# Loading the first layer's weights in two column parts in a deep cross network kernel

## Chip, cores, metric

One core of a Trainium2 chip. The metric is the device time of one execution in microseconds, median over runs. The profile's span is about 1.8 us shorter than that time. Changes of less than 2% (9.5 us here) count as "same"; this study is about fractions of a microsecond at the very start, so single executions are looked at closely.

## The reference

```python
B, Din, L = 16384, 416, 6             # x0: [B, Din], ws: [L, Din, Din], bs: [L, Din], all bfloat16
x = x0
for l in range(L):
    proj = x @ ws[l] + bs[l]
    x = x0 * proj + x
```

## The kernel before

The batch is cut into 8 groups of 2048 rows, a group into 4 chunks of 512. Features lie on partitions: 416 = 3 x 128 + 32, so a layer's output has three full tiles (0, 1, 2) and a tail of 32. TensorE is kept busy by a hand-made order of (group, layer) jobs. A helper, `add(engine, fn, reads, writes, lane)`, derives the semaphore waits from named tokens; a DMA has its own lane and semaphore.

Only the start matters here. SyncE issues every load of it, in this order:

```python
def load_wm(l, eng):                       # 384 rows x 832 B = 312 KB, one DMA
    add(eng, lambda h: h.dma_start(wm[l][:, :, :], ws[l, 0:NT * P, :].rearrange("(t p) f -> p t f", p=P)),
        writes=[("wm", l)], lane=f"wm{l}", batch=0)
...
load_nat(0, 0, 2)                          # rows of chunk 0, first half (208 KB)
load_nat(0, 2, KK)                         # second half
load_wm(0, "sp")
for j in range(1, NJ):                     # rows of chunks 1, 2, 3, in halves
    load_nat(j, 0, 2)
    load_nat(j, 2, KK)
load_w3(0, "sp")                           # the last 32 weight rows, four copies
load_group(1)                              # DMA transposes of the next group
```

The first job, group 0 in layer 0, turns its rows on TensorE, because a DMA transpose would come too late (the first one of this trace, for group 1, is issued at 7.25 us and lands at 12.67):

```python
keep_busy(25, 7)                           # filler matmuls
transposed_chunk(0)                        # 12 transposes, then copies PSUM -> SBUF by VectorE and ScalarE
... biases; keep_busy(5, 3)
full(g, l, 0, ba, True, True, chunks=[0])  # tile 0, chunk 0: first main matmuls, need the weights
full(g, l, 1, bb, True, True, chunks=[0])  # tile 1, chunk 0
transposed_chunk(1)
transposed_chunk(2)
full(g, l, 0, ba, True, True, chunks=[1])
full(g, l, 1, bb, True, True, chunks=[1])
transposed_chunk(3)
transposed_tails(7)
full(g, l, 0, ba, True, True, chunks=[2, 3])
rows32(g, l, 0, ba, False)                 # small rows of tile 0
...                                        # tile 1; then tile 2 for all chunks, tails, second job
```

Of the kernel before, what the change touches and what calls it, by code (L numbers as in the profile page):

```python
# [3 lines left out]
P = 128  # L4
# [17 lines left out]
class Program:  # L22
# [12 lines left out]
    def add(self, eng, fn, reads=(), writes=(), lane=None, batch=None, hold=False, release=False):  # L35
        op = Op(eng, fn, lane, batch)
        deps = {}
        if eng == "pool":
            writes = list(writes) + ["pool"]
        for t in reads:  # L40
            w = self.writer.get(t)
            if w is not None:
                deps[id(w)] = (w, True)
        for t in writes:
            w = self.writer.get(t)
            if w is not None:
                deps[id(w)] = (w, True)
            for r in self.readers.get(t, ()):
                if id(r) not in deps:
                    deps[id(r)] = (r, False)  # L50
        for d, raw in deps.values():
            if d.lane is None and d.eng == eng and lane is None and (eng == "pe" or not raw):
                continue
            op.deps.append(d)
        for t in reads:
            self.readers.setdefault(t, []).append(op)
        for t in writes:
            self.writer[t] = op
            self.readers[t] = []
        if eng == "dve":  # L60
            if hold:
                self.flush()
                self.held = op
            else:
                self.queue[eng].append(op)
                if release:
                    self.flush()
        else:
            self.queue[eng].append(op)
        if lane is not None:  # L70
            batches = self.lanes.setdefault(lane, [])
            if not batches or batches[-1][0] != batch:
                batches.append((batch, []))
            batches[-1][1].append(op)
        return op
# [123 lines left out]
def bass_standalone__cross_network_dcn__recsys_kernel(  # L199
# [6 lines left out]
    B, D = x0.shape  # L206
    L = ws.shape[0]
    NT = 3
# [24 lines left out]
    wm = [nc.alloc_sbuf_tensor(f"wm_{l}", [P, NT, D], BF16) for l in range(L)]  # L233
# [17 lines left out]
    add = pr.add  # L251
# [4 lines left out]
    def x0_tok(s, t, j):  # L256
        return ("x0", s, t, j)
# [7 lines left out]
    def slot(g):  # L265
        return g % NX0

    def bank(b, p0=0, p1=P, n=CH):
        return psum[p0:p1, b * CH:b * CH + n]
# [3 lines left out]
    def take(n):  # L273
        got = [(ring[0] + i) % 8 for i in range(n)]
        ring[0] = (ring[0] + n) % 8
        return got


    def load_wm(l, eng):
        add(eng, lambda h: h.dma_start(wm[l][:, :, :], ws[l, 0:NT * P, :].rearrange("(t p) f -> p t f", p=P)),  # L280
            writes=[("wm", l)], lane=f"wm{l}", batch=0)

    def load_w3(l, eng):
        for j in range(NJ):
            add(eng, lambda h, j=j: h.dma_start(w3[l][j * T32:(j + 1) * T32, :], ws[l, NT * P:D, :]),
                writes=[("w3", l, j)], lane=f"w3{l}", batch=0)

    def load_group(g):
        s = slot(g)
        rows = slice(g * GC, (g + 1) * GC)  # L290
        def turn(t):
            add("sp", lambda h: h.dma_start_transpose(
                x0s[s][:, t * GC:(t + 1) * GC], x0[rows, t * P:(t + 1) * P]),
                writes=[x0_tok(s, t, j) for j in range(NJ)], lane=f"x0_{s}_{t}", batch=g)

        turn(0)
        add("sp", lambda h: h.dma_start_transpose(Tb, x0[rows, D - P:D]),
            writes=[("ost", t, j) for t in range(NT + 1) for j in range(NJ)], lane="Tb", batch=g)
        turn(1)
        turn(2)  # L300
        if g > 1:
            for j in range(NJ):
                q = slice(j * T32, (j + 1) * T32)
                add("sp", lambda h, q=q, j=j: h.dma_start(
                    x0s[s][q, XW:XW + CH], Tb[P - T32:P, j * CH:(j + 1) * CH]),
                    reads=[("ost", 0, 0)], writes=[("x03q", s, j)], lane=f"x03_{s}", batch=g)
            rotate_x03(g)

    def rotate_x03(g):
        s = slot(g)  # L310
        if turn_of(g, 1):
            rotate(x0s[s][:, XW:XW + CH], x0s[s][:, XW + CH:XW + 2 * CH], turn_of(g, 1),
                   x03_toks(s), ("x03r", s), f"x03r_{s}", g)
# [9 lines left out]
    def quad(g, l, j):  # L323
        q = (j + turn_of(g, l)) % NJ
        return q, slice(q * T32, (q + 1) * T32)
# [14 lines left out]
    def x_src(g, l):  # L340

        if l == 0:
            s = slot(g)
            return lambda t, a, b: x0s[s][:, t * GC + a * CH:t * GC + b * CH], lambda t, j: x0_tok(s, t, j)
        s = xset[(g, l)]
        return lambda t, a, b: xs[s][:, t * GC + a * CH:t * GC + b * CH], lambda t, j: ("x", s, t, j)

    def x3_src(g, l):
        if l == 0:
            s = slot(g)  # L350
            return x0s[s][:, XW:XW + CH], x03_toks(s)
        s = xtail[(g, l)]
        return x3s[s][:, :], [("x3", s)]

    def done_with(g, l):
        users[(g, l)] = users.get((g, l), 0) + 1
        if users[(g, l)] < 2:
            return
        if l > 0:
            free_x.append(xset[(g, l)])  # L360
            free_3.append(xtail[(g, l)])
        prefill(g, l + 1)
        if l == L - 1:
            output(g)
            if g == 3:
                load_last()
            if 4 < g + NX0 <= LAST:
                load_group(g + NX0)
# [90 lines left out]
    def full(g, l, i, banks, first, chunk_major, after_chunk=None, chunks=range(NJ), ts_=range(NT)):  # L459
        src, stok = x_src(g, l)  # L460
        ecols = slice(i * P, (i + 1) * P)
        seq = [(t, j) for j in chunks for t in ts_] if chunk_major else \
              [(t, j) for t in ts_ for j in chunks]
        for t, j in seq:
            n = 1
            if (g, l) in HALVES and halves[0] and t != (0 if first else NT - 1):
                halves[0] -= 1
                n = 2
            w = CH // n
            for k in range(n):  # L470
                add("pe", lambda h, t=t, j=j, k=k, w=w: h.matmul(  # L471
                    bank(banks[j])[:, k * w:(k + 1) * w], wm[l][:, t, ecols], src(t, j, j + 1)[:, k * w:(k + 1) * w],
                    start=(first and t == 0), stop=(not first and t == NT - 1)),
                    reads=[stok(t, j), ("wm", l)], writes=[("ps", banks[j])])
            if after_chunk and t == NT - 1:
                after_chunk(j)

# [20 lines left out]
    def tails(batch):  # L498
        bs_ = take(len(batch))
        for (g, l), b in zip(batch, bs_):  # L500
            s3, tok3 = x3_src(g, l)
            for j in range(NJ):
                (ri, qi), (ro, qo) = quad(g, l, j), quad(g, l + 1, j)
                add("pe", lambda h, l=l, b=b, s3=s3, ri=ri, qi=qi, ro=ro, qo=qo: h.matmul(  # L504
                    psum[qo, b * CH:(b + 1) * CH], w3[l][qi, NT * P:D], s3[qi, :],
                    start=True, stop=False, tile_position=(ri * T32, ro * T32)),
                    reads=tok3 + [("w3", l, ri)], writes=[("ps", b)])
        for (g, l), b in zip(batch, bs_):
            src, stok = x_src(g, l)
            for t in range(NT):  # L510
                for j in range(NJ):
                    ro, qo = quad(g, l + 1, j)
                    add("pe", lambda h, t=t, j=j, src=src, l=l, b=b, ro=ro, qo=qo: h.matmul(  # L513
                        psum[qo, b * CH:(b + 1) * CH], wm[l][:, t, NT * P:D], src(t, j, j + 1),
                        start=False, stop=(t == NT - 1), tile_position=(0, ro * T32)),
                        reads=[stok(t, j), ("wm", l)], writes=[("ps", b)])
            evacuate_tail(g, l, b)
        pr.flush()
        for g, l in batch:
            done_with(g, l)  # L520
# [15 lines left out]
    def load_nat(j, k0, k1):  # L536
# [6 lines left out]
        reads=["warm"], writes=["warm"])  # L543
    load_nat(0, 0, 2)
    load_nat(0, 2, KK)
    load_wm(0, "sp")
    for j in range(1, NJ):
        load_nat(j, 0, 2)
        load_nat(j, 2, KK)
    load_w3(0, "sp")  # L550
    load_group(1)

    def second_tails():
# [106 lines left out]
    def job_banks():  # L660
        return take(NJ)
# [159 lines left out]
    for n, it in enumerate(items):  # L821
# [11 lines left out]
        if mode[n] in ("FR", "F1"):  # L833
            banks = job_banks()
# [3 lines left out]
        else:  # L838
            banks = job_banks()
# [13 lines left out]
    g, l = LAST, L - 1  # L853
    src, stok = x_src(g, l)
# [161 lines left out]
```

## Time and profile before

| | before |
|---|---|
| time, median of 3 runs | 475.73 us (475.69 to 475.93) |
| span of the profile | 473.9 us |
| TensorE busy | 467.7 us (99%) |
| TensorE waiting for the first weights | 1.02 us |
| first weights issued, landed | 1.65, 6.08 us |
| first main matmul | 6.21 us |

TensorE is the bound. What can be won by removing a wait is the idle time of TensorE, 6.2 us in all, and the wait for the first weights is the largest item of it inside the stream. The profile lines that show this stand in the prediction.

### The profile page before, as it was taken

Reading aid. Unit: us, or ns where it says so; the run is one execution under the profiler, and the core shown is the slowest. Engines: PE = TensorE matmul, PEld = TensorE weight load, DVE = VectorE, ACT = ScalarE, POOL = GpSimd, SP = SyncE. Lnnn points to the kernel's source line nnn. Section 1 sums busy time; section 2 is a strip of 40 time slices with the busy share of each in tenths; the row PEclk is TensorE's granted clock in tenths of the full one; section 3 lists DMA queues with packets and bytes.
Section 4 is the critical chain, followed back from the end, with each engine's and each line's share of the span. In section 5 each row is a group of like instructions: output and inputs, shape, how many; then the busy total and the mean of one; then the engine's idle time right before and its main releaser. Section 6 shows DMA issues by size and latency. Waiting matters only on the chain.

```text
span 473.9 us, 8467 instructions
## 1 busy us (share of the span) xinstructions
PE 467.7 (99%) x3408; PEld 199.5 (42%) x3408; DVE 404.5 (85%) x700; ACT 340.9 (72%) x371; POOL 6.0 (1%) x15
## 2 busy tenths in 40 slices
PE   8999999999999999999999999999999999999996
PEld 4344445654444444444444444444444444444442
DVE  2888888888888888898888869888888888888897
ACT  4677777777777777777777777777777777777775
POOL 1000000000000000000000000000000000001000
PEclk9999999999999999999999999999999999999999
DMA  8995910740102388369319930880001039026999
GB/s 227 183 183 136 212 46 1 134 90 1 35 0 46 72 233 142 76 151 228 89 25 190 228 92 19 201 247 1 1 10 27 0 61 237 26 46 102 226 173 290
DMA packets 138651, 53.18 MB, mean 112 GB/s; under 512 B 112362, under 2 KB 138100, under 8 KB 138612
## 3 DMA queue, kind: packets, MB, share of 16 engines
q1 hardware_dynamic: 138456, 52.54, 49.8%
q8 instruction: 26, 0.43, 0.4%
q14 instruction: 13, 0.11, 0.1%
q10 hardware_dynamic: 156, 0.11, 0.1%
HBM read 5.97 MB, written 13.63 MB: 41 GB/s over the span
## 4 chain that ended last, share of the span: by engine, by line
PE 94%; DMA 2%; DVE 2%; ACT 1%; SPq 0%; issue 0%; DVEq 0%
PE ps L471 78%; PE ps L492 7%; PE ps L513 7%; PE ps L486 1%; DMA wm<-in_ws_dram 1%; DVE x L931 1%; DVE x L925 1%; DMA x<-x 1%; ACT tw L398 1%; PE ps L504 1%; DMA ot<-x 1%; PE ps L591 0%; DVE tw L407 0%; SPq L537 0%; ACT ost L709 0%
## 5 line engine op out<-in xcount | busy, mean ns | idle before, releaser
L398 ACT ACTIVATE tw<-ps,bias 128x1024 bf16<-128x1024 f32 (+1 forms) x295 | 299.5, 1070 | 119.8 <-PE ps L492 80.1
L471 PE MATMUL ps<-x,wm 128*128 128x512 bf16 (+1 forms) x1755 | 379.6, 372 | 1.0 <-DMA wm<-in_ws_dram 1.0
L471 PEld LDWEIGHTS ps<-x,wm 128*128 128x128 bf16 x1755 | 165.1, 98 | 209.7 <-issue 28.2
L407 DVE TENSOR_TENSOR tw<-tw,x 128x1024 bf16<-128x1024 bf16 (+1 forms) x285 | 192.6, 683 | 52.5 <-ACT tw L398 52.0
L412 DVE TENSOR_TENSOR x<-tw,x 128x1024 bf16<-128x1024 bf16 (+1 forms) x285 | 182.4, 680 | 0.0
L492 PE MATMUL ps<-x,w 32*128 32x512 bf16 x512 | 39.2, 379 | 0.0
L513 PE MATMUL ps<-x,wm 128*32 128x512 bf16 x564 | 33.0, 380 | 0.0
L438 ACT ACTIVATE ts<-ps,bias 128x512 bf16<-128x512 f32 x47 | 28.7, 700 | 0.0
L442 DVE TENSOR_TENSOR x<-ts,x 128x512 bf16<-128x512 bf16 x47 | 18.6, 417 | 3.2 <-DMA x<-x 3.1
L513 PEld LDWEIGHTS ps<-x,wm 128*32 128x32 bf16 x564 | 13.8, 96 | 17.5 <-issue 5.2
L492 PEld LDWEIGHTS ps<-x,w 32*128 32x128 bf16 x512 | 7.8, 92 | 26.9 <-issue 26.4
L440 DVE TENSOR_TENSOR ts<-ts,x 128x512 bf16<-128x512 bf16 x47 | 18.5, 417 | 0.0
L711 POOL COPY ost<-ot 128x512 bf16<-128x512 bf16 x6 | 4.6, 766 | 422.9 <-DMA ot<-x 422.9
L867 PE MATMUL ps<-wm,x 128*128 128x416 bf16 x48 | 9.7, 340 | 0.0
L601 DVE COPY x<-ps 128x512 bf16<-128x512 bf16 x5 | 2.0, 422 | 8.6 <-PE ps L591 8.5
L919 ACT ACTIVATE x<-ps 128x416 bf16<-128x416 f32 x16 | 7.7, 517 | 2.1 <-PE ps L867 2.0
L603 ACT ACTIVATE x<-ps 128x512 bf16<-128x512 bf16 x7 | 3.8, 595 | 5.3 <-PE ps L591 5.3
L867 PEld LDWEIGHTS ps<-wm,x 128*128 128x128 bf16 x48 | 4.2, 98 | 4.4 <-issue 1.0
L504 PE MATMUL ps<-x,w 32*32 32x512 bf16 x188 | 5.9, 374 | 0.0
L486 PE MATMUL ps<-x,w 32*32 32x512 bf16 x208 | 5.7, 385 | 0.0
L931 DVE TENSOR_TENSOR x<-x,x 128x832 bf16<-128x832 bf16 (+1 forms) x9 | 4.7, 540 | 0.2
L925 DVE TENSOR_TENSOR x<-x,x 128x832 bf16<-128x832 bf16 (+1 forms) x10 | 4.8, 498 | 0.0
(40 smaller groups left out, 32.3 us busy)
## 6 DMA issues: line engine op xcount, KB each, us to landing
out_dram<-ost SPq DMA_DIRECT2D x6, 1664.0 KB, 7.0
x<-x SPq DMA_DIRECT2D x24, 96.0 KB, 2.1
wm<-in_ws_dram SPq DMA_DIRECT2D x6, 312.0 KB, 3.3
x<-in_x_dram SPq DMA_DIRECT2D x8, 208.0 KB, 4.2
x<-in_x_dram SPq DMA_DIRECT2D x4, 416.0 KB, 8.3
out_dram<-ost SPq DMA_DIRECT2D x2, 832.0 KB, 5.4
x<-x SPq DMA_DIRECT2D x22, 64.0 KB, 2.0
out_dram<-x SPq DMA_DIRECT2D x3, 416.0 KB, 4.3
```

The costliest lines, as they stand in the source:

```text
L398: add("act", lambda h, a=a, w=w, b0=b0: h.activation(tw[r][:, a * CH:(a + w) * CH], psum[:, b0 * CH:(b0 + w) * CH], ACT_F.Identity, bias=b ...
L407: add("dve", lambda h, a=a, e=e: h.tensor_tensor(tw[r][:, a * CH:e * CH], tw[r][:, a * CH:e * CH], x0s[s0][:, i * GC + a * CH:i * GC + e * ...
L412: add("dve", lambda h, a=a, e=e: h.tensor_tensor(xs[so][:, i * GC + a * CH:i * GC + e * CH], tw[r][:, a * CH:e * CH], src(i, a, e), ALU.ad ...
L438: add("act", lambda h: h.activation(ts[r][:, :], bank(b), ACT_F.Identity, bias=bias[:, 3, l:l + 1], scale=1.0), reads=[("ps", b), "bias"], ...
L440: add("dve", lambda h: h.tensor_tensor(ts[r][:, :], ts[r][:, :], x03, ALU.mult), reads=[("ts", r)] + tok0, writes=[("ts", r)], release=True)
L442: add("dve", lambda h: h.tensor_tensor(x3s[so][:, :], ts[r][:, :], res, ALU.add), reads=[("ts", r)] + rtok, writes=[("x3", so), ("x3", so, ...
L471: add("pe", lambda h, t=t, j=j, k=k, w=w: h.matmul(bank(banks[j])[:, k * w:(k + 1) * w], wm[l][:, t, ecols], src(t, j, j + 1)[:, k * w:(k ...
L486: add("pe", lambda h, q=q, j=j, r=r, c=c, o=o: h.matmul(psum[o, banks[j] * CH:(banks[j] + 1) * CH], w3[l][q, i * P + c * T32:i * P + (c + ...
L492: add("pe", lambda h, q=q, j=j, r=r: h.matmul(bank(banks[j]), w3[l][q, ecols], src[q, :], start=first and not inner, stop=not first and no ...
L504: add("pe", lambda h, l=l, b=b, s3=s3, ri=ri, qi=qi, ro=ro, qo=qo: h.matmul(psum[qo, b * CH:(b + 1) * CH], w3[l][qi, NT * P:D], s3[qi, :], ...
L513: add("pe", lambda h, t=t, j=j, src=src, l=l, b=b, ro=ro, qo=qo: h.matmul(psum[qo, b * CH:(b + 1) * CH], wm[l][:, t, NT * P:D], src(t, j, ...
L867: add("pe", lambda h, t=t: h.matmul(bank(b, n=D), xcol(t, j, kk), wm[l][:, t, :], start=(first and t == 0), stop=(not first and t == NT - 1)),
```

## The change

The intent: output tiles 0 and 1 need 256 of the 416 weight columns. Load those first, and let the other 160 come behind the rows, so that the first matmuls and the rows of chunks 1 to 3 have less ahead of them.

```diff
-    def load_wm(l, eng):
-        add(eng, lambda h: h.dma_start(wm[l][:, :, :], ...),
-            writes=[("wm", l)], lane=f"wm{l}", batch=0)
+    W0 = 2 * P
+    def load_wm(l, eng, f0=0, f1=D):
+        toks = {0: [("wm", l)], W0: [("wm", l, "rest")]}[f0] if l == 0 else [("wm", l), ("wm", l, "rest")]
+        add(eng, lambda h: h.dma_start(
+            wm[l][:, :, f0:f1], ws[l, 0:NT * P, f0:f1].rearrange("(t p) f -> p t f", p=P)),
+            writes=toks, lane=f"wm{l}_{f0}", batch=0)
+    def wm_tok(l, i):
+        return ("wm", l) if i < 2 else ("wm", l, "rest")
 # in full() and tails(): reads ("wm", l) -> wm_tok(l, i)
-    load_wm(0, "sp")
+    load_wm(0, "sp", 0, W0)
     for j in range(1, NJ):
         load_nat(j, 0, 2)
         load_nat(j, 2, KK)
     load_w3(0, "sp")
+    load_wm(0, "sp", W0, D)
     load_group(1)
```

More of the change, by code (lines that the diff above doesn't have):

```diff
@@ L276, in take @@
         return got
-    def load_wm(l, eng):
-        add(eng, lambda h: h.dma_start(wm[l][:, :, :], ws[l, 0:NT * P, :].rearrange("(t p) f -> p t f", p=P)),
-            writes=[("wm", l)], lane=f"wm{l}", batch=0)
+    W0 = 2 * P
[6 more added lines that the diff above has]
+        return ("wm", l) if i < 2 else ("wm", l, "rest")
     def load_w3(l, eng):
@@ L473, in full @@
                     start=(first and t == 0), stop=(not first and t == NT - 1)),
-                    reads=[stok(t, j), ("wm", l)], writes=[("ps", banks[j])])
+                    reads=[stok(t, j), wm_tok(l, i)], writes=[("ps", banks[j])])
             if after_chunk and t == NT - 1:
@@ L515, in tails @@
                         start=False, stop=(t == NT - 1), tile_position=(0, ro * T32)),
-                        reads=[stok(t, j), ("wm", l)], writes=[("ps", b)])
+                        reads=[stok(t, j), wm_tok(l, NT)], writes=[("ps", b)])
             evacuate_tail(g, l, b)
```

## The prediction

> **What bounds the kernel now.** I read the page's busy times first, then the groups, then the chain of waits, then the waits of TensorE, and last the order of time of the first 25 us.
>
> ```profile
> span 473.9 us, 8467 instructions
> PE 467.7 (99%) x3408; PEld 199.5 (42%) x3408; DVE 404.5 (85%) x700; ACT 340.9 (72%) x371; POOL 6.0 (1%) x15
> L471 PE MATMUL ps<-x,wm 128*128 128x512 bf16 (+1 forms) x1755 | 379.6, 372 | 1.0 <-DMA wm<-in_ws_dram 1.0
> ```
>
> TensorE (PE) is busy for 467.7 of 473.9 us, so only 6.2 us can be won by removing waits. The last line names the one wait of any size inside the stream: 1.0 us before the main matmuls, released by the load of the first layer's weights. The chain of waits shows the same piece at the very start:
>
> ```profile
> 1.65 4.43 DMA wm<-in_ws_dram
> 6.08 0.14 issue
> 6.21 1.46 PE ps L471 x6
> 7.67 1.34 PE ps L591 x24
> ```
>
> The weights (one DMA of 312 KB, issued at 1.65) land at 6.08, and 0.13 us later the first real matmul starts. From there on the chain is PE work nearly without a break until the last 20 us, so whatever the first matmul gains is kept to the end, unless a later wait takes it back. TensorE and the SyncE queue in order of time:
>
> ```profile
> 4.74 0.45 PE L573 MATMUL ps<-const-bfloat16-1.0 128*128 128x512 bf16 x2
> 6.21 1.46 PE L471 MATMUL ps<-x,wm 128*128 128x512 bf16 x6 [1.02 <-DMA wm<-in_ws_dram]
> ...
> 0.73 0.88 SPq L537 DMA_DIRECT2D x<-in_x_dram  x2
> 1.65 0.78 SPq L280 DMA_DIRECT2D wm<-in_ws_dram  x1
> 2.48 2.86 SPq L537 DMA_DIRECT2D x<-in_x_dram  x6
> 5.38 1.82 SPq L285 DMA_DIRECT2D w<-in_ws_dram  x4
> 7.25 2.32 SPq L292 DMA_TRANSPOSE x<-in_x_dram  x1
> ```
>
> The filler matmuls end at 5.19; the gap up to 6.21 is the 1.02 us. The SyncE queue has no gap from 0.73 to past 18 us: chunk 0 (2 loads of 208 KB), weights, chunks 1 to 3 (6 loads), the four small weight rows, then the DMA transposes of group 1. One instruction more in the middle pushes all that follows. How full the DMA engines are:
>
> ```profile
> core 0: us, PE busy (x) PEld busy (x) DVE busy (x) ACT busy (x) POOL busy (x), PEclk, DMA share, GB/s
> 3.20:4.40 1.20, 1.20 (x15) 0.81 (x13) 0.00 (x0) 0.00 (x0) 0.00 (x0) 1.00 0.74 151
> 4.40:5.20 0.80, 0.79 (x12) 0.35 (x9) 0.42 (x1) 0.62 (x2) 0.31 (x1) 1.00 0.98 320
> 5.20:6.20 1.00, 0.00 (x0) 0.01 (x1) 0.00 (x0) 0.55 (x2) 0.13 (x1) 1.00 1.03 376
> ```
>
> From 4.4 us the engines are saturated (320 to 376 GB/s): the front is limited by DMA throughput, and bytes taken out of it make everything behind land earlier.
>
> [...] the packets' median is 39 ns for 832 B and 69 ns for 1664 B, so 30 ns for 832 B more and 9 ns fixed. [...] The new pieces have rows of 512 B and 320 B; no run yet shows 320 B, but the 256 B packets of the transposes have a median of 18 ns, on the same straight line, so I expect no cliff. [...] the granted clock is 1.00 throughout, so no clock effect is to be had or lost.
>
> **The change part by part.** Removed ahead of the first matmul: 160 of 416 weight columns, 384 rows x 320 B = 120 KB. Added: one DMA with 384 rows of 320 B behind the four small weight rows, a semaphore, and a wait on it before output tile 2. Later layers are unchanged: one DMA writes both names.
>
> *Step 1, first part lands earlier.* 384 rows over 16 engines are 24 packets each. Before: 24 x 39 ns = 0.94 us. With 512 B a packet costs, by the line above, 9 + 512 x 0.036 = 27.5 ns (estimate), 24 of them 0.66 us: 0.28 us less. From the rate, 120 KB at 376 GB/s is 0.33 us. The remaining 3.5 us of the 4.43 us are issue, queueing behind chunk 0 and slow first packets, and stay. So the first matmul starts at about 5.9: a gain g of 0.3 us, not the whole 1.02. It could not start before 5.2 anyway (filler), and its third matmul needs a ScalarE copy ending at 5.66.
>
> *Step 2, rows of chunks 1 to 3.* They queue behind the same weights and land about 0.3 us earlier too. The tightest is the second half of chunk 2: issued at 3.96, landed 4.3 us later at 8.25; its transposes ran at 8.51 (the trace's single instructions). That is 0.16 us of slack after the landing's own 0.1 us, plus 0.3: it allows a gain of about 0.45, so it does not bind at g = 0.3 but caps a larger one.
>
> *Step 3, the rest of the weights.* Issued at about 7.25, landing some 4.3 us later (as the small rows at that place, 4.2 us): 11.6. Tile 2 starts at 14.43 with the small rows and at 14.97 with these weights: about 3 us of slack, no wait.
>
> *Step 4, the price.* The transposes of group 1 are pushed. The issue of such a weight load took 0.43 to 0.78 us, plus 0.04 us between issues; in engine time both parts cost 24 x (27.5 + 20.5 - 39) = 0.22 us more than the whole. So the last transpose, issued at 15.76 and landing 4.6 us later at 20.38, comes d = 0.2 to 0.8 us later, central 0.55. Who waits: the second job (16 main matmuls from 18.76) reads the third row block of group 1 with its thirteenth matmul, which started at 21.36. Slack now: 21.36 - 20.38 - 0.13 = 0.85 us. With g + d = 0.85 it is used up exactly. PE keeps min(g, 0.85 - d): 0.3 at d = 0.55, 0.05 at d = 0.8.
>
> *Step 5, further on.* The second row block lands at 17.87 and is read at 20.50: ample. The second layer's weights land at 21.70 and are needed after 24.6; the next group's transposes are needed much later. Nothing else binds; the end moves with PE.
>
> Sum: 475.73 - 0.3 + about 0.05 for the uncertain wait of step 4 = 475.5 us.
>
> **The rivals.** *A: the whole 1.02 us is won (474.7).* For: weights are the only thing the first matmul waits for, and the copies are ready. Against: the load's 4.43 us are mostly not bytes, and step 2 allows hardly 0.5. I give it one chance in ten. *B: the wait moves to the last transpose of group 1 (475.7 to 476.2).* For: the SyncE queue is gapless, its 0.85 us of slack is as large as gain and push together, and the transposes' issues vary by themselves (2.0 to 3.1 us each). Against: at their start the engines are still busy with row loads, so part of the push may vanish in queueing that exists anyway. Three in ten that it takes most of the gain, one in ten that it costs more than the gain. *C: the first part lands no earlier*[...] (475.7 or a little worse). For: the 3.2 to 4.4 stretch was only 74% busy, with single packets far above the median. Against: from 4.4 to its landing the queue was full. One in seven. *D: 320 B rows are much dearer than the line says*: it would add to d only and ends like B.
>
> **Range and chances.** g from 0 to 0.7 and d from 0.2 to 1.0 give a net gain between -0.2 and +0.7 us; the runs before spread by 0.24 us. So 475.0 to 475.95 should hold it 8 times in 10. A 2% change is 9.5 us, while all PE idle time is 6.2 us, most of it at the end: no path leads there short of a failure.
>
> **What would show it.** Right: the wait on the weights before the main matmuls falls from 1.02 to about 0.7 us and stays the front's only one; first main matmul near 5.9; first issue still 384 packets, now of 512 B at about 27 ns; SyncE's first transpose issue at 7.7 to 8.0; no PE wait for the rest of the weights. Step 4 is wrong if PE shows a wait on the transposed rows near 21 us (rival B) by more than 0.1 us; step 1 if the first matmul starts at 5.5 or before (A) or at 6.1 or later (C); step 2 if the transposes of chunk 2 wait. The prediction as a whole is wrong if the time leaves the range, above all through a wait after 25 us that I did not see.

475.73 - 0.3 + 0.05 = 475.5 us, where the 0.3 comes from the packets' medians (39 and 69 ns) and the rate of 376 GB/s, and the 0.05 from the issue times and landings of before. That no clock effect was to be had was my estimate; it rests on the column PEclk alone, which the next section corrects.

## The result

| | before | after |
|---|---|---|
| median, 6 runs each of the same job | 475.84 us (475.69 to 476.56) | 475.77 us (475.56 to 476.2) |
| span of the profile | 473.9 | 474.4 |
| first weights issued, landed | 1.65, 6.08 | 1.65, 6.42 |
| first main matmul | 6.21 | 6.55 |

The ratio of the fast runs is 0.9997, 95% interval 0.9984 to 1.001: the same. (A ratio is the mean time of one kernel's fast runs over that of the other's of the same rounds, so not quite the ratio of the medians quoted here.) The time lies in the predicted range, but the profile contradicts the first step: the smaller part landed 0.34 us later than the whole had. The chain of waits of the changed kernel, with start, duration and work:

```profile
1.65 4.76 DMA wm<-in_ws_dram
6.42 0.14 issue
6.55 1.46 PE ps L479 x6
```

TensorE in order of time, and the SyncE queue, also of the changed kernel:

```profile
5.31 0.71 PE L582 MATMUL ps<-const-bfloat16-1.0 128*128 128x512 bf16 x2
6.55 1.46 PE L479 MATMUL ps<-x,wm 128*128 128x512 bf16 x6 [0.53 <-DMA wm<-in_ws_dram]
...
1.65 0.43 SPq L284 DMA_DIRECT2D wm<-in_ws_dram  x1
2.13 3.17 SPq L545 DMA_DIRECT2D x<-in_x_dram  x6
5.34 1.82 SPq L293 DMA_DIRECT2D w<-in_ws_dram  x4
7.20 0.43 SPq L284 DMA_DIRECT2D wm<-in_ws_dram  x1
7.68 2.73 SPq L300 DMA_TRANSPOSE x<-in_x_dram  x1
```

Three things differ. The wait has halved, from 1.02 to 0.53 us, and yet the matmul starts later: the wait is shorter only because the fillers before it ended at 6.02 instead of 5.19. TensorE ran at half its clock for longer in this execution; the trace's clock records grant the full clock from 6.28 us on, against 3.48 before. (The column PEclk of the views doesn't show this: it prints 1.00 wherever the trace has no clock record, and there is none ahead of the first grant. The half clock is read from the matmuls: of 128x512, they start 0.215 us apart at full clock, and 0.43 us apart ahead of the grant, as the fillers of both kernels from 1.15 to 2.86 us, and the main matmuls of late_whole, below.) Second, the landing moved by 0.34 us the wrong way. Third, the delay is handed through: matching the two kernels' 3408 weight loads on TensorE one by one, the changed kernel's are 0.33 us late from the first main matmul, and stay within 0.08 us of that to the end. So what happens before the first job's end decides the rest. (TensorE busy reads 463.0 us there instead of 467.7 because 54 matmul records are missing; that is no work saved.)

One profile of each kernel cannot tell an effect from an execution's luck, and these two were far apart by luck: the profiled execution of before was the fastest of its six (475.69), that of after the slowest (476.2). So the first experiments repeat both.

### The profile page after: what moved, and what is told of

Its sections match the earlier page's. It is cut to its first block, busy times and chain, and to the rows that moved or that the text cites. A ratio compares the mean times of both kernels' runs of the same rounds, so it can differ in the third digit from the quotient of the medians.

```text
span 474.4 us, 8414 instructions
## 1 busy us (share of the span) xinstructions
PE 463.0 (98%) x3354; PEld 200.0 (42%) x3408; DVE 404.5 (85%) x700; ACT 341.2 (72%) x371; POOL 6.6 (1%) x15
## 3 DMA queue, kind: packets, MB, share of 16 engines
HBM read 5.97 MB, written 13.63 MB: 41 GB/s over the span
## 4 chain that ended last, share of the span: by engine, by line
PE 92%; DMA 2%; DVE 2%; ACT 2%; issue 1%; SPq 0%; DVEq 0%
PE ps L479 77%; PE ps L500 7%; PE ps L521 6%; ACT tw L406 2%; DMA wm<-in_ws_dram 1%; PE ps L494 1%; DVE x L940 1%; DMA x<-x 1%; DVE x L934 1%; PE ps L512 1%; DMA ot<-x 1%; DVE tw L415 0%; PE ps L600 0%; SPq L545 0%; DVE x L610 0%
## 5 line engine op out<-in xcount | busy, mean ns | idle before, releaser
L479 PE MATMUL ps<-x,wm 128*128 128x512 bf16 (+1 forms) x1701 | 372.1, 371 | 6.2 <-issue 3.7
```

The costliest lines, as they stand in the source:

```text
L479: add("pe", lambda h, t=t, j=j, k=k, w=w: h.matmul(bank(banks[j])[:, k * w:(k + 1) * w], wm[l][:, t, ecols], src(t, j, j + 1)[:, k * w:(k ...
```

## The experiments

Twelve kernels, in three jobs of four, each with five rounds; every job has 11 runs of the kernel before beside it. My theories were *bytes* (the landing follows the bytes ahead, as predicted), *stalls* (slow packets decide it) and *two gates* (the rows of chunk 2 stand right behind the weights, so TensorE follows the later of the two). A *gate* is anything that TensorE has to wait for at the start. A letter b or a in a name stands for the kernel before or the changed one.

### Both kernels again

No edit.

> The kernel before, unchanged, to see how much one execution differs from another. First profile: weights landed at 6.08 us, first main matmul at 6.21. If the landing is a fixed sum (theory bytes), this execution lands within 0.1 us of it. If it hangs on a few slow packets (theory stalls), it moves by 0.2 us or more. Time 475.7 to 476.1 either way, ratio 1.000.

> The changed kernel, unchanged. Its first profile had the first part landing at 6.42 us, 0.34 later than the whole before, against the 0.3 earlier that I predicted. Theory bytes: that was an outlier, and this execution lands at about 5.8, some 0.3 ahead of the kernel before. Theory stalls: it lands anywhere from 5.7 to 6.5, not clearly ahead. Theory competition (the rows of chunk 1 start 0.35 us sooner behind the shorter issue and share the engines with it): again 6.3 to 6.5. In each case the first main matmul follows the landing by 0.13 us, and the span is that start plus 467.7 us within 0.2 us.

Measured: b_again median 475.62 us, ratio 1.0007 (0.9992 to 1.0022), one run at 477.83; a_again 475.61, ratio 0.9999 (0.9987 to 1.0011). The kernel before had a median of 475.69. The weights landed at 5.66 in b_again and 5.64 in a_again: no lead for the smaller part. The same kernel's landing moved by 0.42 us (6.08 to 5.66) between two executions, the changed one's by 0.78 (6.42 to 5.64). The 0.28 us that I had worked out lies inside that. Theory competition, which wanted 6.3 to 6.5 in a_again too, has failed; and in b_noN, below, chunk 1's rows were issued as early as in the changed kernel (at 2.13), and the whole load landed at 5.39.

b_again shows something else. The weights came early, but that was not what TensorE then waited for. The chain of waits:

```profile
3.93 4.35 DMA x<-in_x_dram
8.28 0.05 issue
8.32 0.51 PE ps L591 x6
```

and TensorE's weight loads (PEld) in the same profile:

```profile
6.87 1.21 PEld L591 LDWEIGHTS ps<-ident,x 128*128 128x128 bf16 x18
8.32 0.34 PEld L591 LDWEIGHTS ps<-ident,x 128*128 128x128 bf16 x6 [0.24 <-DMA x<-in_x_dram]
```

The second half of chunk 2's rows, issued at 3.93, landed at 8.28, and the last six of 24 transposes had to wait for it. In the first profile of the same kernel these rows landed at 8.25 and were not waited for, as TensorE came only at 8.46. The view of TensorE's matmuls hides such short waits, because a matmul's modelled end covers them (the list of the matmuls' waits in b_again names no DMA at all); the weight loads show them. In a_again there is a third kind of wait, between the first main matmuls:

```profile
5.75 0.13 PEld L479 LDWEIGHTS ps<-x,wm 128*128 128x128 bf16 x2 [0.45 <-ACT x L612]
6.16 0.58 PEld L479 LDWEIGHTS ps<-x,wm 128*128 128x128 bf16 x4 [0.28 <-ACT x L612]
```

The third matmul waits for ScalarE's copy of chunk 0. These copies end at 5.66 and 5.64 in the two profiles of before, and at 6.21 and 6.11 in those of after, where the half clock lasted until 6.28 and 4.75 us and slowed the transposes ahead of the copies (in after, two groups of six took 0.83 and 0.84 us, in before 0.54 and 0.51). All profiles with chunk 0's rows at their usual place agree: the last copy ends at 5.60 to 5.75 us where the full clock came by 3.76, at 5.92 to 6.11 where it came at 4.35 to 4.75, and at 6.21 where it came at 6.08 or later.

### Much fewer bytes in the first part

```diff
-    load_wm(0, "sp", 0, W0)
+    add("dve", lambda h: h.memset(wm[0][:, :, 64:W0], 0.01), writes=[("wm", 0)])
+    ...dma_start(wm[0][:, :, 0:64], ws[0, 0:NT*P, 0:64]...), writes=[("wm", 0)]
```

> Wrong result on purpose: the first part loads 64 columns instead of 256 (384 rows of 128 B, the rest of the tile's columns set to a constant by VectorE). Bytes ahead of the first matmul fall from 192 to 48 KB. Theory bytes: 24 packets an engine at some 14 ns instead of 27, and 144 KB at 376 GB/s, so it lands 0.3 to 0.4 us earlier than the changed kernel's typical landing (about 5.5 if that is 5.8). Theory stalls: the 384 packets still meet the same slow ones; landing stays at 5.7 to 6.4, with a few 128 B packets of 300 to 1200 ns in the trace.

Measured: median 475.46 us, ratio 0.9995 (0.9983 to 1.0007); the runs' medians differ by 0.23. The comparison with the reference passed in spite of the false weights, which says how tolerant it is, not that the result is right. The part landed at 4.93 us, 0.7 ahead of a_again, with a single slow packet of 128 B. So, in this one profile, bytes do matter when three quarters are cut, and stalls alone do not describe it. The rows behind gained nothing that shows: the second half of chunk 2 landed at 8.04 with 264 KB less ahead of it than in before, where the four profiles with the whole load have 7.77 to 8.28. And TensorE got little of it. It began at 5.52, then waited for chunk 2's rows (landed 8.04, transposes at 8.08), and then for a wait that I had feared as rival B, on the third block of group 1's transposes. TensorE's weight loads:

```profile
20.05 0.53 PEld L479 LDWEIGHTS ps<-x,wm 128*128 128x128 bf16 x3
21.07 0.55 PEld L479 LDWEIGHTS ps<-x,wm 128*128 128x128 bf16 x4 [0.49 <-DMA x<-in_x_dram]
```

That block landed at 21.03. It cost TensorE some 0.1 to 0.2 us (456.49 us from the small rows to the end in the table further below, against 456.2 to 456.4 elsewhere), less than the 0.49 the weight load waited, since a weight load runs ahead of its matmul (by 0.21 us in the median of before).

### Touching the weights early

```diff
+    add("act", lambda h: h.dma_start(touch[:, :, :], ws[0, 0:NT * P, 0:16].rearrange(...)), ...)
     add("act", lambda h: h.dma_start(brow[0:L, :], bs[:, :]), ...)
```

> The changed kernel with one small load more on ScalarE's queue at 0.7 us, 32 B of each of the same 384 weight rows into a scratch tile. Theory stalls by first touch (the slow packets are the first reads of the weights' memory by each engine): the slow packets move to this small load, those of 512 B over 200 ns all but vanish, and the first part lands at 5.2 to 5.7. Theory stalls by time (whatever runs at 3.5 to 5 us is slow): 512 B packets over 200 ns remain about ten, landing 6.0 to 6.5. Theory bytes: no earlier, 0.1 us later. Time: 0.3 to 0.6 us less under first touch, else the same within 0.2 us.

Measured: median 475.72 us, ratio 1.0001 (0.9989 to 1.0013); landing 5.97. There were 13 packets of 512 B above 200 ns between 3 and 6 us, the longest 1141 ns. First touch is out, as far as 32 B of each row can tell: the small load read the same rows from 2.56 to 3.09 us without one slow packet (9 ns each), and the large one met them all the same.

### Taking one gate away

Two kernels without the wait for chunk 2's rows (its transposes read chunk 1's rows, as do chunk 3's), and two without the wait for the weights (chunk 0 is multiplied by a constant tile). All loads stay as they were.

```diff
# noN
-    x0n[:, j, k, t * P:(t + 1) * P] ... reads=[("nat", j, k), ...]
+    x0n[:, min(j, 1), k, t * P:(t + 1) * P] ... reads=[("nat", min(j, 1), k), ...]
# noW
+    add("dve", lambda h: h.memset(wm[L - 1][:, :, 0:2 * P], 0.01), writes=[("wm", L - 1)])
-    full(g, l, 0, ba, True, True, chunks=[0])        # and tile 1
+    full(g, l, 0, ba, True, True, chunks=[0], fake=L - 1)
```

> Kernel before, with the transposes of chunks 2 and 3 reading the rows of chunk 1 (wrong result on purpose; all loads stay). So TensorE no longer waits for the second half of chunk 2's rows, which in its second profile landed at 8.28 us and held its transposes to 8.32, while the weights had landed at 5.66. Theory two gates (TensorE goes by the later of weights and chunk 2 rows, and the two are about equally late): first main matmul 0.13 us after the landing, the second half of chunk 2's transposes exactly 2.27 us after the first weight load of TensorE, and the time 0.1 to 0.2 us under the kernel before (475.5 to 475.6 for 475.7). Theory weights only: no change (under 0.05 us).

> The same on the changed kernel: only the weights gate is left. Theory bytes with two gates: the first part lands on average 0.28 us before the whole, so this is 0.2 to 0.3 us faster than b_noN, unless the third block of group 1's transposes then holds TensorE near 21 us (it may take back 0.1 to 0.2). Theory stalls: same as b_noN within 0.1 us.

> Kernel before, with the 6 main matmuls of chunk 0 using a weight tile that VectorE fills with a constant (wrong result on purpose; all loads stay). The first wait on the weights is gone altogether. Theory two gates: the first main matmul starts at 5.3 to 5.8, but the second half of chunk 2's transposes still starts at 8.2 to 8.4, right behind its rows, so the time falls by no more than 0.1 to 0.15 us. Theory weights only (the 1.0 us is worth 1.0): first main matmul at 5.3 and a time 0.5 us lower or more.

> The same on the changed kernel: only the rows of chunk 2 gate. Theory bytes with two gates: with 120 KB less ahead of them these rows land 0.3 us sooner than in b_noW (near 7.95) and the time is 0.3 us under it. Theory stalls: landing within 0.15 us of that in b_noW, same time.

Measured, with the kernel before at 475.80 us in this job:

| | median | ratio (95%) | weights landed | chunk 2, second half landed |
|---|---|---|---|---|
| b_noN | 475.58 | 1.0004 (0.9985 to 1.0023) | 5.39 | 7.96, not waited for |
| a_noN | 475.38 | 0.9990 (0.9978 to 1.0003) | 5.42 | 7.70, not waited for |
| b_noW | 475.63 | 0.9995 (0.9982 to 1.0007) | 5.31, not waited for | 7.77 |
| a_noW | 475.41 | 0.9992 (0.9978 to 1.0006) | 5.84, not waited for | 8.03 |

(b_noN's mean is drawn up by runs at 477.95 and 476.62. The noN kernels are wrong by a relative error of 0.34, as intended.) The wait that reads 1.02 us in the first profile is worth under 0.2 us in the medians when it is removed outright: b_noW against before, 475.63 against 475.80. The interval of the ratio reaches down to 0.9982, 0.86 us, so the times exclude a gain of 1.02 us but not one of 0.5. Theory weights only, which wanted 0.5 us or more, is contradicted by the median and by the profile: no load was waited for, and the small rows of tile 0 (table further below) still started at 12.44, against 12.70 and 12.49 in the two profiles of before. Taking away the other gate brought about as much (475.58), within the same noise. Where I was wrong: I expected chunk 2's rows to hold b_noW to 8.2 to 8.4. They landed at 7.77. There, TensorE had the half clock until 6.08, the copies ended at 6.21, and its main matmuls were late through that, not through any load. The third gate did the work of the second.

In both pairs the changed variant is 0.2 us lower. That agrees in sign with bytes, but with six runs each and intervals 0.0025 (1.2 us) wide or wider it is not shown to be more than chance, and the landings of these pairs do not carry it: 5.39 against 5.42 for the weights where only they gate, 7.77 against 8.03 for the rows where only those do.

How far the engines got in the first microseconds explains these landings better than the kernel does. The stretch from 3.0 to 4.4 us in all eight profiles of unaltered load order: before, b_again, b_noN, b_noW, then after, a_again, a_noN, a_noW. The last two columns are the DMA engines' busy share and GB/s.

```profile
3.00:4.40 1.40, 1.40 (x16) 0.81 (x14) 0.00 (x0) 0.00 (x0) 0.00 (x0) 1.00 0.77 182
3.00:4.40 1.40, 1.40 (x16) 0.89 (x14) 0.00 (x0) 0.00 (x0) 0.00 (x0) 1.00 0.74 187
3.00:4.40 1.40, 1.40 (x12) 1.06 (x11) 0.00 (x0) 0.00 (x0) 0.00 (x0) 1.00 0.83 244
3.00:4.40 1.40, 1.40 (x12) 1.06 (x11) 0.00 (x0) 0.00 (x0) 0.00 (x0) 1.00 0.89 264
```

```profile
3.00:4.40 1.40, 1.40 (x12) 0.94 (x11) 0.00 (x0) 0.00 (x0) 0.00 (x0) 1.00 0.89 171
3.00:4.40 1.40, 1.40 (x12) 0.94 (x11) 0.00 (x0) 0.00 (x0) 0.00 (x0) 1.00 0.87 224
3.00:4.40 1.40, 1.40 (x12) 1.03 (x11) 0.00 (x0) 0.00 (x0) 0.00 (x0) 1.00 0.84 244
3.00:4.40 1.40, 1.40 (x16) 0.98 (x14) 0.00 (x0) 0.00 (x0) 0.00 (x0) 1.00 0.74 198
```

With the whole load, 182, 187, 244 and 264 GB/s go with landings at 6.08, 5.66, 5.39 and 5.31 us. With the part, 171, 198, 224 and 244 GB/s go with 6.42, 5.84, 5.64 and 5.42. The more was moved, the earlier the landing, in both kernels. Between the best and the worst stretch of before lie (264 - 182) GB/s x 1.4 us = 115 KB, as much as the 120 KB that the change moves out of the way, so a swing of this size can hide its gain. It isn't the whole of it: at one rate, 244 GB/s, the part should have led, and landed at 5.42 against 5.39. (More bytes moved and an earlier landing are also nearly the same thing said twice.) The average of the four is even later for the part (5.83 against 5.61), which with such a spread means nothing.

The packets of these eight traces show where the gain is and where it goes. Half of the 384 weight packets had ended at 4.51, 4.52, 4.21 and 4.11 us with the whole load, and at 4.10, 3.86, 3.78 and 3.98 with the part: every one earlier, by 0.41 us on average. Nine tenths had ended at 4.62 to 5.13 and at 4.61 to 5.59, the last at 5.01 to 5.74 and at 5.09 to 6.10: no lead is left. The landing comes some 0.3 us after the end of the last packet (0.34 in before, 0.32 in after), and by that end 150 to 234 packets of the rows behind had already begun in the changed kernel (85 to 173 in before). So fewer bytes do bring most of the part in sooner, and its last few packets give the lead away. Why these come late isn't shown.

### A dose in the other direction

```diff
-    load_wm(0, "sp")
     for j in range(1, NJ):
         load_nat(j, 0, 2)
         load_nat(j, 2, KK)
+        if j == 1:
+            load_wm(0, "sp")
```

> Kernel before, with its whole weight load moved behind the two loads of chunk 1's rows: a dose in the other direction. The weights have 416 KB more ahead of them, some 1.1 us, so they land at 6.4 to 7.2 instead of 5.3 to 6.1; the rows of chunk 2 keep their place (7.8 to 8.3). Theory two gates, and no slack behind them: the end follows the weights one to one from where the two gates cross, so the time rises by 0.5 to 0.9 us (476.2 to 476.6). Theory that something later (group 1's transposes, the tail) hides delays at the start: rise under 0.2 us.

Measured: median 478.10 us (476.46 to 479.17), ratio 1.0042 (1.0026 to 1.0059), against 475.74. The direction is right and the size is not: some 2.0 us of mean loss where I expected 0.5 to 0.9. The weights landed at 7.02, as expected. TensorE in order of time shows what I had left out:

```profile
5.30 0.71 PE L574 MATMUL ps<-const-bfloat16-1.0 128*128 128x512 bf16 x2
7.16 2.72 PE L471 MATMUL ps<-x,wm 128*128 128x512 bf16 x6 [1.14 <-DMA wm<-in_ws_dram]
```

The six main matmuls took 2.72 us instead of 1.46: the half clock lasted until 9.91 us. The wait here cost its length and then work at half speed: the small rows of tile 0 started at 14.98, 2.28 us after those of before, and this run (478.01) is as much slower. Whether the wait is what kept the full clock back is not shown; I see the two together in this one profile. Of the other five runs the record has only the time and the mean granted clock, 0.994 in two (479.17 and 478.22 us) and 0.998 or 0.999 in the rest; that mean leaves out the time before the first clock record (the profiled run has 0.998, where half the clock for 9.91 of its 476.2 us would make 0.990 at most).

### Weights first of all, and weights on a second queue

```diff
# wm_first
+    load_wm(0, "sp", 0, W0)
     load_nat(0, 0, 2)
     load_nat(0, 2, KK)
-    load_wm(0, "sp", 0, W0)
# act_first
-    load_wm(0, "sp", 0, W0)
+    load_wm(0, "act", 0, W0)        # ahead of the bias load on ScalarE's queue
```

> The changed kernel, with the first part ahead of chunk 0's rows too. Weights land at about 3.5 to 4.2, chunk 0's rows some 0.5 us later than now (4.4 to 4.6), so the copies of chunk 0 end near 6.1 to 6.3 and take over as the gate of the first matmuls (5.6 to 5.9); chunk 2's rows have the same bytes ahead and land as now (7.7 to 8.3). Theory two gates: time as the changed kernel within 0.15 us. On the slow packets: if they belong to the weights' rows, 512 B packets over 200 ns stand near 2 us; if to the time 3.5 to 5 us, they are now 1664 B packets there.

> The changed kernel, with the first part issued by ScalarE at 0.7 us, in parallel with chunk 0's rows on SyncE's queue. It shares the engines with them: weights at 3.8 to 4.6, chunk 0's rows at 4.0 to 4.6, SyncE's later issues 0.5 us earlier. Theory two gates: the rows of chunk 2 stay at 7.6 to 8.2 because the engines carry the same bytes, so 0 to 0.2 us under the changed kernel. Theory issue-bound (SyncE's issues space the rows): rows of chunk 2 land 0.4 us sooner and the time falls by 0.3 us or more.

Measured: wm_first 477.71 us (476.46 to 478.65), ratio 1.0037 (1.0024 to 1.005), a miss; I had expected no change. The weights landed at 3.32, but the second half of chunk 0's rows only at 5.59 (3.98 before), 1.0 us after what I had expected, and TensorE stood idle for 0.31 and 0.70 us before the transposes of these rows, as its matmuls show. (The profile is of the fastest of the six runs, 476.46. It explains that one, 0.7 us; what cost the median another 1.2 us was not profiled.)

```profile
3.91 0.82 PE L600 MATMUL ps<-ident,x 128*128 128x128 bf16 x6 [0.31 <-DMA x<-in_x_dram]
5.64 0.51 PE L600 MATMUL ps<-ident,x 128*128 128x128 bf16 x6 [0.70 <-DMA x<-in_x_dram]
```

Between 3 and 6 us there were 27 packets above 200 ns, all of 1664 B: rows of x. In the first profile of before these were 15 of 832 B and 2 of 1664 B. In act_first the weight packets ran from 2.63 to 3.47 us, none over 27 ns, and 19 packets of rows were over 200 ns. So the slow packets do not belong to the weights; in these three profiles what was in flight then was hit. Whether it is the time that counts, or the third load on the queue, is left open.

act_first: 475.63 us, ratio 0.9997 (0.9985 to 1.0009), the same. Its weights landed at 3.86 and chunk 2's rows at 7.43, earlier than in any other profile, as theory issue-bound wanted; yet the time did not fall by 0.3 us. Chunk 0's rows came at 4.47 and its copies ended at 6.38, so the third gate held the start at 5.94.

### Chunk 2's second half later in TensorE's order

```diff
     transposed_chunk(1)
-    transposed_chunk(2)
+    transposed_chunk(2, (0,), False)     # first half, no copies yet
     full(... chunks=[1]) x2
+    transposed_chunk(2, (2,))            # second half, then the copies
     transposed_chunk(3)
```

> The changed kernel with TensorE's order changed: the second half of chunk 2's transposes comes after the main matmuls of chunk 1, 1.3 us later, so that gate is gone (right result). Theory two gates: as a_noN, 0.1 to 0.2 us under the changed kernel (475.4 for 475.6), with TensorE's weight loads following the first one without a hold until 9 us, except that chunk 1's matmuls may wait up to 0.15 us for their copies. Theory weights only: same as the changed kernel or 0.1 us worse.

Measured: 475.90 us (475.66 to 475.95), ratio 1.0002 (0.999 to 1.0014), 0.16 above before in the same job (475.74) and 0.3 above a_again's median of another, and not below either. The gate is gone (nothing waits for these rows), but the copies now lie where they are waited for. From the first main weight load to the small rows of tile 0 this profile took 7.07 us (5.64 to 12.71), against 6.51 when nothing but the weights gates: 0.56 us of new waits. TensorE's weight loads:

```profile
8.54 0.76 PEld L479 LDWEIGHTS ps<-x,wm 128*128 128x128 bf16 x5 [0.23 <-DVE x L610]
11.19 0.33 PEld L479 LDWEIGHTS ps<-x,wm 128*128 128x128 bf16 x3 [0.23 <-ACT x L612]
12.17 0.11 PEld L479 LDWEIGHTS ps<-x,wm 128*128 128x128 bf16 x2 [0.34 <-ACT x L612]
```

None of the versions beats both kernels by more than the spread.

### The gates put together

In the twelve profiles of this table the small rows of tile 0 start at about one fixed distance behind whichever gate came last: 6.61 us after the landing of the weights (read from before, after and pretouch, where they bind), 4.21 us after the landing of chunk 2's second half (from b_again), 6.12 us after the last copy of chunk 0 (from wm_first). From there to the last weight load of a matmul it is 456.2 to 456.5 us in all twelve, however early they are. late_whole and t2_late are left out: their first job runs at half clock for longer, or in another order. Times in us; a dash is a gate that the kernel lacks.

| profile | weights + 6.61 | chunk 2 + 4.21 | copies + 6.12 | latest gate | small rows started |
|---|---|---|---|---|---|
| before | 12.69 | 12.46 | 11.78 | weights | 12.70 |
| b_again | 12.27 | 12.49 | 11.76 | chunk 2 | 12.49 |
| b_noN | 12.00 | - | 12.09 | copies | 12.09 |
| b_noW | - | 11.98 | 12.33 | copies | 12.44 |
| after | 13.03 | 12.96 | 12.33 | weights | 13.03 |
| a_again | 12.26 | 12.17 | 12.23 | weights, copies | 12.26 |
| a_noN | 12.03 | - | 12.04 | copies, weights | 12.04 |
| a_noW | - | 12.24 | 11.72 | chunk 2 | 12.24 |
| narrow_first | 11.54 | 12.25 | 12.07 | chunk 2 | 12.26 |
| pretouch | 12.59 | 12.37 | 11.87 | weights | 12.59 |
| act_first | 10.47 | 11.64 | 12.50 | copies | 12.49 |
| wm_first | 9.93 | 12.41 | 13.39 | copies | 13.39 |

Every row but b_noW fits within 0.02 us (there, the first main matmul itself still ran at half clock; its six took 1.60 us instead of 1.46). Five of the rows gave the three distances, so the test is in the other seven, of which six fit. Each gate binds somewhere, and within one kernel it changes from one execution to the next. This is the two gates theory with a third gate added.

## Why the prediction was right, and where not

The number was right: 475.5 predicted, 475.77 measured, in the range. That was in good part luck: the range held the time of no change at all (475.73), so the number could hold whether step 1 did or not. Over all jobs, the unaltered kernels have medians of 475.73 (before with b_again, 45 runs) and 475.72 (after with a_again, 11 runs). The reasons were right in part.

**Step 1, the first part lands 0.28 us earlier: failed.** The packet costs were right; the changed kernel's medians are 27 ns for 512 B and 20 ns for 320 B, against 27.5 and 20.5 estimated; so rival D, dear 320 B rows, is out. What failed is "the remaining 3.5 us ... stay". They do not stay: the DMA rate at 3.0 to 4.4 us runs from 171 to 264 GB/s, and landings with it over 0.8 us or more (5.31 to 6.08 for the whole, 5.42 to 6.42 for the part). Nor were the engines full from 4.4 us on, as I had read from one execution; the changed kernel's first profile has

```profile
4.40:5.20 0.80, 0.80 (x14) 0.59 (x11) 0.29 (x1) 0.08 (x1) 0.00 (x0) 1.00 0.53 163
```

against 0.98 and 320 GB/s. And the 0.28 us assumed that the last packet gains what the others gain; half of the packets were in 0.41 us earlier on average, the last ones were not. By my own sign (6.1 or later) the first matmul at 6.55 spoke for rival C; a_again's, at 5.78, for neither. I had read the 74% busy share of that stretch as an argument for rival C and given it one chance in seven. C as I meant it, that bytes don't set the landing at all, falls too, since 48 KB landed at 4.93. A gain of the calculated size may be there on average; medians that are 0.07, 0.2 and 0.2 us lower in three pairs point to it, the fourth (a_again) is 0.08 under before and 0.01 under b_again, and nothing here proves it. Open is also another thing that I only saw in passing: of 57 runs of kernels with the whole load at its old place five took over 476.5 us (up to 477.95), of 43 with the part behind chunk 0's rows or earlier (wm_first left out) none; five of five on one side would come about once in 18 by chance. No profile caught such a run.

**Step 2, chunk 2's rows land 0.3 us earlier too: not seen; that they cap the gain: right, and more important than I made it.** Their second half landed at 8.25, 8.28, 7.96 and 7.77 with the whole load ahead, at 8.75, 7.96, 7.70 and 8.03 with the part: 8.07 and 8.11 on average. As for the cap, I gave it as a cap on gains above 0.45 us. It is a gate at the same height as the weights, and binds in b_again already in the kernel before. I missed the third gate: I named the copy that ends at 5.66 as a lower limit, but did not ask whether it can move. It moves to 6.21 with the clock.

**Step 3, no wait for the rest: right.** The rest landed at 11.21 in the first profile of after, 10.64 in the second; its users start more than 3 us later, and no wait shows.

**Step 4, the price on group 1's transposes: right in kind, over-sized.** I expected the last of them 0.2 to 0.8 us later. It landed at 20.38 and 20.46 before, and at 20.50 and 20.17 after: no delay of that size (with b_noN, b_noW, a_noN and a_noW, so four profiles each, it is 20.07 and 20.20 on average). One reason is in the queue lines: the first issue took 0.43 us where it had taken 0.78, which paid for most of the second issue. The extra 0.2 to 0.4 us falls on one issue of the front in half of the profiles: on the weights in before, b_again, b_noW and narrow_first, on a row load in after, pretouch and late_whole, on none in the others. As narrow_first is a version of the changed kernel, the change doesn't do away with it. The wait I feared did appear in narrow_first.

**Step 5, the end moves with TensorE: right.** The fixed 456.2 to 456.5 us shows it.

**Rival A (the whole 1.02 us) is refuted** by b_noW: with the wait gone, under 0.2 us of it shows in the medians, and the interval ends at 0.86. Where the expected gain went, then: to the last packets of the part, into a choice among three gates of nearly the same height, and below the spread of the first loads. The granted clock was not "1.00 throughout", as I had read from the column PEclk: in before itself it is full only from 3.48 us on. And "no clock effect is to be had or lost" holds for these two kernels as far as their four profiles show it (a load is the latest gate in each, in a_again level with the copies), but not further: in the profile of late_whole six matmuls at half clock alone took 1.26 us more.

## What to carry to other kernels

A wait that the profile puts at 1.0 us is worth only what lies between it and the next gate (b_noW: under 0.2 us in the medians); list every gate of the stretch with its distance to a common later point, and take the lead of the latest over the second latest as the most that removing it can bring (in the profile of before 12.69 - 12.46 = 0.23 us). For a start-up effect of a few tenths, profile each kernel several times first, since here the same load of one kernel landed up to 0.78 us apart in two executions, more than the change could bring. And look at weight loads, not matmuls, for short waits on TensorE (0.24 us in b_again, which the matmuls don't show).

## What else the traces show, and what stays open

- The clock records of before, b_again, after and a_again grant the full clock first at 3.48, 3.64, 6.28 and 4.75 us, in kernels that give TensorE the same work up to there. What sets the moment isn't shown.
- In late_whole TensorE had worked from 0.77 to 6.01 us without a gap, a wait of 1.14 us followed, and the half clock lasted until 9.91; six matmuls took 2.72 us instead of 1.46. I had taken a gap of 1.02 us to be harmless to the clock, which was not shown. Whether such a gap matters ahead of the first grant, this one profile doesn't settle.
- Packets of the loads to SBUF in before and after have medians of 20 ns at 320 B, 27 at 512, 39 at 832 and 69 at 1664, which lie on one line, with a fixed share of some 9 ns a packet (estimate from these medians). No cliff showed between 320 and 1664 B.
- The first loads have a slow stretch: 171 to 264 GB/s at 3.0 to 4.4 us in the same load order, with single packets of 512 B of up to 1211 ns (in after) where the median is 27. Its cause is open; pretouch speaks against first touch of the memory.
